# Float16 attention tiles as pairs of 64x64 products, with queries and values split as they lie

## The chip, the cores and the metric

One Trainium2 chip, one of its cores. The metric is the device time of one execution in microseconds; three executions of the kernel before are shown, and one more was taken with the profiler.

## What is computed

Attention within chunks of 64 tokens, then two feed-forward parts on its output (8 batches, 8 heads, 576 tokens, head size 64, model size 512). Cut to what matters:

```python
q_c = q.reshape(B, H, nc, 64, D); k_c, v_c likewise          # nc = 9 chunks
scores = scale * q_c @ k_c.transpose(0, 1, 2, 4, 3)           # 64 x 64 per batch, head and chunk
attn = softmax(scores); out = attn @ v_c
...
h = relu(x @ w_in); u, v = halves of h                        # first part, model size 512 -> 1024
gated = u * (w_spatial @ layernorm(v) + b_spatial); x = gated @ w_out
...
u = x + (x^T U V)^T                                           # second part
return u + relu(u @ w_ch1) @ w_ch2                            # 512 -> 2048 -> 512
```

Inputs and result are float32.

## The kernel before

Values of float32 are split into a float16 part and a float16 remainder, and a product of two such values is the sum of three float16 products: high by high, high by low, low by high. The helper `mm3` (lines 150 to 155) issues these three; each has its own weight load.

The attention has 36 tiles. A tile holds two chunks (c = 0 on partitions 0 to 63, c = 1 on partitions 64 to 127) with all 8 heads. Tiles 0 to 8 (`gen_first`) stay in float32 and are computed as pairs of 64x64 products: queries, keys and values lie on the partitions of their half, and a matmul takes partitions 0 to 63 or 64 to 127 for weights, data and output. Tiles 9 to 35 (`gen_attn`) are float16. For them the queries are written into a block-diagonal tile `qbd` (a 128x128 block per head that holds the 64x64 block of each half on its diagonal and zeros elsewhere), the values into `vbd` in the same manner, and one 128x128 weight load and one matmul with 64 moving columns serve both halves: 8 heads by 3 terms, 24 matmuls for the scores (`sp`, lines 541 to 543) and 24 for the weighted sum (`o`, lines 563 to 567). The zeros are written once, by two memsets on GpSimd (lines 888 to 891), ahead of which VectorE writes one element of each tile so that the memset waits for the seventh weight block (`after`, line 219).

`a_split_qk` and `a_split_v` (lines 358 to 379) fill these tiles: ScalarE casts the float16 part, GpSimd subtracts it for the remainder. For `qbd` and `vbd` there is one cast and one subtraction per half, of 64 partitions by 512 elements; for the keys `kd` one of each on 128 partitions. `qbd`, `vbd` and `kd` have one buffer, so the split of the next tile waits for the last matmul on this one. The row maxima, differences and sums of the softmax run on VectorE, the exponential on ScalarE; the probabilities `ph` go through a transposing DMA to `pt` and are the moving operand of the weighted sum.

Around it, `gen_dec` and `next_rest` decode the weights (loads, a scaling on ScalarE, three bit operations on VectorE at lines 183 to 187, a cast on ScalarE, a subtraction on GpSimd at line 195); `gen_moe` is the first feed-forward part, `gen_ch` the second (`phid` and `acc`). `Flow` walks the generators in a planned order of time that is set by costs such as `mmcost`; after that a scheduler orders each engine's instructions with its own model of their times. The one pin that concerns the attention is on the first score matmul of tiles 9 to 17.

Of the kernel before, what the change touches and what calls it, by code (L numbers as in the profile page):

```python
# [9 lines left out]
F16 = mybir.dt.float16  # L10
# [3 lines left out]
ALU = mybir.AluOpType  # L14
# [3 lines left out]
B, H, S, E = 8, 8, 576, 64  # L18
# [29 lines left out]
def mmcost(n, k=1):  # L48
    return k * (n / 2.4 + 2.7)
# [53 lines left out]
def moe_kernel(  # L103
# [12 lines left out]
    nc = tc.nc  # L116
    NT = q.shape[0]

    const = ctx.enter_context(tc.tile_pool(name="const", bufs=1))
# [22 lines left out]
    v4 = const.tile([128, S], F16, name="v4")  # L142
    vt2 = const.tile([128, 2, D], F16, name="vt2")
    mhalf = const.tile([128, 1], F32, name="mhalf")
    qbd = const.tile([128, 2, H, 2, 64], F16, name="qbd")
    vbd = const.tile([128, 2, 4, 2, 2, 64], F16, name="vbd")

    fl = Flow()

    def mm3(o, wh, wl, xh, xl, start, stop, pin=False):  # L150
        m = nc.tensor.matmul(out=o, lhsT=wh, rhs=xh, start=start, stop=False)  # L151
        if pin:
            tc.keep_in_program_order(m)
        nc.tensor.matmul(out=o, lhsT=wh, rhs=xl, start=False, stop=False)  # L154
        nc.tensor.matmul(out=o, lhsT=wl, rhs=xh, start=False, stop=stop)  # L155


    stage = {}

# [59 lines left out]
    def after(n, t):  # L219

        nc.vector.tensor_copy(out=t[0:1, 0:1], in_=wt[n][0:1, 1, 3, 127:128])
# [125 lines left out]
    def a_load(upto):  # L347
        while nload[0] <= min(upto, NT - 1):
            i = nload[0]
            qk = sb.tile([128, 2, 512], F32, tag="ld4", name="qk", bufs=3)  # L350
            vf = sb.tile([128, 512], F32, tag="ldv", name="vf", bufs=1)
            nc.sync.dma_start(out=qk[:, 0, :], in_=q[i])
            nc.sync.dma_start(out=qk[:, 1, :], in_=k[i])
            nc.sync.dma_start(out=vf, in_=v[i])
            ld[i] = (qk, vf)
            nload[0] += 1

    def a_split_qk(i):
        qk, vf = ld[i]
        kd = sb.tile([128, 2, H, 64], F16, tag="kd", name="kd", bufs=1)  # L360
        qv = qk[:, 0, :].rearrange("p (h t) -> p h t", h=H)
        kv = qk[:, 1, :].rearrange("p (h t) -> p h t", h=H)
        for c in range(2):
            r = slice(c * 64, (c + 1) * 64)
            nc.scalar.copy(out=qbd[r, 0, :, c, :], in_=qv[r])  # L365
            nc.gpsimd.tensor_tensor(  # L366
                out=qbd[r, 1, :, c, :], in0=qv[r], in1=qbd[r, 0, :, c, :], op=ALU.subtract)
        nc.scalar.copy(out=kd[:, 0], in_=kv)
        nc.gpsimd.tensor_tensor(out=kd[:, 1], in0=kv, in1=kd[:, 0], op=ALU.subtract)
        spl[i] = kd  # L370

    def a_split_v(i):
        vf = ld.pop(i)[1]
        nc.scalar.activation(out=vf, in_=vf, func=ACTF.Copy, scale=4.0)
        vf = vf.rearrange("p (a c e) -> p a c e", a=4, c=2)
        for c in range(2):
            r = slice(c * 64, (c + 1) * 64)
            nc.scalar.copy(out=vbd[r, 0, :, :, c, :], in_=vf[r])  # L378
            nc.gpsimd.tensor_tensor(out=vbd[r, 1, :, :, c, :], in0=vf[r], in1=vbd[r, 0, :, :, c, :], op=ALU.subtract)  # L379

    def put_tail(b):
        j = b % 2
# [3 lines left out]
    def a_softmax(sp, se=None):  # L386
        mx = sb.tile([128, H, 1], F32, tag="mx", name="mx", bufs=4)
        nc.vector.tensor_reduce(out=mx, in_=sp, op=ALU.max, axis=AXX)
        if se is None:
            se = sb.tile([128, H, 64], F32, tag="se", name="se", bufs=2)  # L390
        nc.vector.tensor_tensor(out=se, in0=sp, in1=mx.to_broadcast([128, H, 64]), op=ALU.subtract)
        nc.scalar.activation(out=se, in_=se, func=ACTF.Exp, scale=0.125)
        return se

    def a_norm(sp, se, scale):
        sm = sp[:, :, 0:1]
        nc.vector.tensor_reduce(out=sm, in_=se, op=ALU.add, axis=AXX)
        nc.vector.tensor_scalar(out=sm, in0=sm, scalar1=1e-9, scalar2=scale, op0=ALU.add, op1=ALU.mult)
        nc.vector.reciprocal(out=sm, in_=sm)
        nc.vector.tensor_tensor(out=se, in0=se, in1=sm.to_broadcast([128, H, 64]), op=ALU.mult)  # L400

    def a_out(i, o):
        p, r = divmod(i, 9)
        b = 2 * p + (r > 4)
        if r != 4:
            st = r if r < 4 else r - 5
            t0 = st * 128
            if st == 0:
                xT[b] = sb.tile([128, 2, 4, S], F16, tag="xT", name="xT", bufs=2)
                if r == 5:  # L410
                    put_tail(b)
            x = xT[b]
            nc.scalar.copy(out=x[:, 0, :, t0:t0 + 128], in_=o)
            nc.vector.tensor_tensor(
                out=x[:, 1, :, t0:t0 + 128], in0=o, in1=x[:, 0, :, t0:t0 + 128], op=ALU.subtract
            )
            fl.done(("x", b, st), 1500.0)
            return
        x = xd[p] = sb.tile([128, 2, 4, 128], F16, tag="xd", name="xd", bufs=1)
        nc.scalar.copy(out=x[:, 0], in_=o)  # L420
        nc.vector.tensor_tensor(out=x[:, 1], in0=o, in1=x[:, 0], op=ALU.subtract)
        fl.done(("x", 2 * p, 4), 2500.0)
        put_tail(2 * p)
# [100 lines left out]
    def gen_attn(lo, hi):  # L524
        if lo == 9:
            nload[0] = 9
            a_load(9)
            a_split_qk(9)
            a_split_v(9)
        for i in range(lo, hi):  # L530
            r = i % 9
            b = 2 * (i // 9) + (r > 4)
            a_load(i + 1)

            if i < 18:
                yield "until", 45000.0 + 16000.0 * (i - 9)
            kd = spl.pop(i)
            pin = True
            sp = ps_a.tile([128, H, 64], F32, tag="a", name="sp")
            qm = qbd.rearrange("p a h c t -> p a h (c t)")  # L540
            for h in range(H):
                mm3(sp[:, h, :], qm[:, 0, h, :], qm[:, 1, h, :], kd[:, 0, h, :], kd[:, 1, h, :], True, True,
                    i < 18 and h == 0)
            se = a_softmax(sp)
            if i + 1 < NT:
                a_split_qk(i + 1)
            yield "pe", mmcost(64, 24)
            yield "wait", WA
            a_norm(sp, se, float(2 ** -8))
            ph = sb.tile([128, 2, 512], F16, tag="ph", name="ph", bufs=1)  # L550
            sef = se.rearrange("p h j -> p (h j)")
            nc.scalar.copy(out=ph[:, 0, :], in_=sef)
            nc.gpsimd.tensor_tensor(out=ph[:, 1, :], in0=sef, in1=ph[:, 0, :], op=ALU.subtract)
            pt = sb.tile([128, 2, 4, 128], F16, tag="pt", name="pt", bufs=1)
            nc.sync.dma_start_transpose(
                out=pt.rearrange("p a b t -> p (a b) t"), in_=ph.rearrange("p a n -> p (a n)")
            )
            yield "wait", WB
            if r in (0, 5) and b > 1:
                yield "need", ("win", b - 2)  # L560
            o = ps_a.tile([128, 4, 128], F32, tag="a", name="o")
            vm = vbd.rearrange("p a b c x e -> p a b c (x e)")
            for hp in range(4):
                for c in range(2):
                    tt = slice(c * 64, (c + 1) * 64)
                    mm3(o[:, hp, tt], vm[:, 0, hp, c, :], vm[:, 1, hp, c, :], pt[:, 0, hp, tt], pt[:, 1, hp, tt],
                        True, True)
            a_out(i, o)
            if i + 1 < NT:
                a_split_v(i + 1)  # L570
            yield "pe", mmcost(64, 24)
            yield "wait", WC
# [291 lines left out]
    def all_of(g):  # L864
        for kind, val in g:
            if kind == "pe":
                tick(val)
# [17 lines left out]
    nc.gpsimd.memset(sp_t2, 0.0)  # L885
    nc.gpsimd.memset(u_l, 0.0)
    nc.gpsimd.memset(u_h, 0.0)
    for t in (qbd, vbd):
        u = t.rearrange("p a b c d -> p (a b c d)") if len(t.shape) == 5 else t.rearrange("p a b c d e -> p (a b c d e)")
        after(7, u)  # L890
        nc.gpsimd.memset(t, 0.0)
    all_of(gen_dec(1))
    moe = gen_moe(0)
    moe1 = None
# [16 lines left out]
    fl.t = 0.0  # L911
    fl.ev = {n: 0.0 for n in fl.ev}
    fl.add(gen_attn(9, NT), pace=0.0)

    def rest():
# [77 lines left out]
```

## Time and profile before

| | |
|---|---|
| median of three executions | 1298.79 us (1296.63 to 1301.45) |
| profiled execution | 1298.71 us, span 1296.9 us |
| TensorE matmuls busy | 1251.6 us, 97% of the span, 8612 matmuls and as many weight loads |
| VectorE, ScalarE, GpSimd busy | 507.3, 500.2, 504.5 us |
| chain that ended last | TensorE 80%, VectorE 7%, DMA 5%, GpSimd 4%, ScalarE 2%, issue 2% |
| granted TensorE clock, mean | 0.987 |

The span runs from the first to the last instruction; the 1.8 us between it and the execution's time lie around it. A matmul's row gives its start and a duration that includes the way through the array, so matmuls overlap in the rows and their distance from start to start is what the engine's time is made of. The chain is followed back from the last instruction; where it passes through an engine, that engine set the time there.

### The profile page before, as it was taken

To read this page: it belongs to the slowest core of one execution; us is meant where nothing else is said; L and a number is where in the kernel's file an instruction comes from. 1 tells how busy PE (TensorE), PEld (TensorE's weight loads), DVE (VectorE), ACT (ScalarE), POOL (GpSimd) and SP (SyncE) were. 2 spreads that over 40 slices of the span, in tenths; PEclk is the share of its full clock that TensorE was granted. 3 is DMA by queue.
4 is the path that set the end of the run, shared out by engine and by line. 5 is a ranking of instruction groups with operands and counts; after the bars stand their busy time and mean duration, and the time that the engine had idled before them with its cause. 6 is when DMAs were issued, how large, how long until landed. Compare 5 with 4: busy or idle time off the path is not lost.

```text
span 1296.9 us, 21079 instructions
## 1 busy us (share of the span) xinstructions
PE 1251.6 (97%) x8612; PEld 708.7 (55%) x8612; DVE 507.3 (39%) x934; ACT 500.2 (39%) x1024; POOL 504.5 (39%) x630
## 2 busy tenths in 40 slices
PE   7798997999999999999999999999999999999998
PEld 4476554445665466645665466545654565444443
DVE  7885777545333633242233513241114211221211
ACT  4655556445454444433354324332123212221110
POOL 4765767637455555524365515222112211020000
PEclk8799998999999999999999999999999999999999
DMA  9445335522233322420123101200011001000000
GB/s 344 154 129 137 120 115 134 123 83 53 66 78 65 90 58 50 93 67 5 34 73 71 50 1 26 45 33 5 1 28 42 1 1 28 26 17 1 33 1 33
DMA packets 95369, 81.46 MB, mean 63 GB/s; under 512 B 69668, under 2 KB 70308, under 8 KB 95272
## 3 DMA queue, kind: packets, MB, share of 16 engines
q1 hardware_dynamic: 94120, 75.92, 21.4%
q10 hardware_dynamic: 1152, 4.19, 1.0%
q8 instruction: 67, 1.10, 0.4%
q14 instruction: 30, 0.25, 0.1%
HBM read 53.62 MB, written 9.44 MB: 49 GB/s over the span
## 4 chain that ended last, share of the span: by engine, by line
PE 80%; DVE 7%; DMA 5%; POOL 4%; ACT 2%; issue 2%; SPq 0%; DVEq 0%; POOLq 0%; ACTq 0%
PE acc L151 9%; PE phid L151 9%; PE phid L155 9%; PE phid L154 9%; PE acc L155 9%; PE acc L154 9%; PE pb L151 7%; PE pb L155 7%; PE pb L154 7%; DVE dt L184 2%; DVE dt L187 2%; DMA wch<-in_q_dram 1%; DMA tr<-tr 1%; DVE dt L183 1%; POOL wch L195 1%
## 5 line engine op out<-in xcount | busy, mean ns | idle before, releaser
L824 DVE SCALAR_TENSOR_TENSOR hid<-phid,hid 128x512 f16<-128x512 f32 x144 | 99.2, 689 | 356.4 <-ACT hid L822 356.1
L151 PE MATMUL phid<-uT,wch 128*128 128x512 f16 x576 | 218.6, 379 | 1.1 <-DVE x L786 0.6
L154 PE MATMUL phid<-uT,wch 128*128 128x512 f16 x576 | 218.6, 379 | 0.0
L155 PE MATMUL phid<-uT,wch 128*128 128x512 f16 x576 | 218.4, 379 | 0.0
L154 PE MATMUL acc<-hid,wch 128*128 128x512 f16 x576 | 218.3, 379 | 0.0
L155 PE MATMUL acc<-hid,wch 128*128 128x512 f16 x576 | 218.3, 379 | 0.0
L151 PE MATMUL acc<-hid,wch 128*128 128x512 f16 x576 | 207.9, 379 | 2.2 <-ACT hid L822 2.2
L155 PEld LDWEIGHTS <-wch 128*128 128x128 f16 x1152 | 112.8, 98 | 131.4 <-issue 0.3
L151 PEld LDWEIGHTS <-wch 128*128 128x128 f16 x1152 | 112.7, 98 | 122.4 <-issue 6.5
L154 PEld LDWEIGHTS <-wch 128*128 128x128 f16 x1152 | 112.8, 98 | 117.8 <-issue 1.7
L822 ACT ACTIVATE hid<-phid 128x512 f16<-128x512 f32 x144 | 85.4, 594 | 179.7 <-PE phid L155 179.5
L683 POOL TENSOR_TENSOR gt<-g,gt 128x288 f16<-128x288 f32 x64 | 49.3, 772 | 151.7 <-ACT gt L681 151.4
L379 POOL TENSOR_TENSOR vbd<-vf,vbd 64x512 f16<-64x512 f32 x54 | 63.9, 1183 | 91.0 <-ACT vbd L378 83.7
L749 POOL TENSOR_TENSOR tr<-x,tr 128x64 f16<-128x64 f32 x64 | 48.1, 773 | 93.1 <-issue 52.1
L366 POOL TENSOR_TENSOR qbd<-qk,qbd 64x512 f16<-64x512 f32 x54 | 62.3, 1154 | 52.1 <-ACT qbd L365 48.3
L151 PE MATMUL pb<-sp_m,vn 128*128 128x288 f16 x256 | 73.2, 286 | 2.8 <-DVE hid L824 1.5
L154 PE MATMUL pb<-gt,w 128*128 128x288 f16 x256 | 73.7, 288 | 2.1 <-POOL gt L683 2.1
L151 PE MATMUL pb<-gt,w 128*128 128x288 f16 x256 | 73.5, 288 | 1.8 <-ACT tr L746 1.7
L151 PE MATMUL pb<-xT,w 128*128 128x288 f16 x256 | 73.5, 287 | 0.7 <-ACT up L659 0.7
L155 PE MATMUL pb<-gt,w 128*128 128x288 f16 x256 | 73.6, 288 | 0.0
L154 PE MATMUL pb<-xT,w 128*128 128x288 f16 x256 | 73.5, 287 | 0.0
L155 PE MATMUL pb<-xT,w 128*128 128x288 f16 x256 | 73.5, 287 | 0.0
(177 smaller groups left out, 2224.9 us busy)
## 6 DMA issues: line engine op xcount, KB each, us to landing
st<-in_wk_dram SPq DMA_DIRECT2D x24, 512.0 KB, 4.0
out_dram<-ot SPq DMA_DIRECT2D x32, 256.0 KB, 2.0
vf<-in_v_dram SPq DMA_DIRECT2D x27, 256.0 KB, 2.7
qk<-in_q_dram SPq DMA_DIRECT2D x27, 256.0 KB, 2.7
qk<-in_k_dram SPq DMA_DIRECT2D x27, 256.0 KB, 3.0
room<-in_wk_dram SPq DMA_DIRECT2D x8, 512.0 KB, 7.2
wch<-in_wk_dram ACTq DMA_DIRECT2D x8, 512.0 KB, 4.3
wch<-in_q_dram SPq DMA_DIRECT2D x9, 256.0 KB, 6.3
```

Of the source, the lines that this page charges most:

```text
L151: m = nc.tensor.matmul(out=o, lhsT=wh, rhs=xh, start=start, stop=False)
L154: nc.tensor.matmul(out=o, lhsT=wh, rhs=xl, start=False, stop=False)
L155: nc.tensor.matmul(out=o, lhsT=wl, rhs=xh, start=False, stop=stop)
L183: nc.vector.tensor_scalar(out=tb, in0=tb, scalar1=3, scalar2=None, op0=ALU.logical_shift_left)
L184: nc.vector.scalar_tensor_tensor(out=tb, in0=w[:, 0::2], scalar=29, in1=tb, op0=ALU.logical_shift_right, op1=ALU.bitwise_or)
L187: nc.vector.scalar_tensor_tensor(out=tb, in0=w[:, 1::2], scalar=0x80000000, in1=tb, op0=ALU.bitwise_and, op1=ALU.bitwise_or)
L366: nc.gpsimd.tensor_tensor(out=qbd[r, 1, :, c, :], in0=qv[r], in1=qbd[r, 0, :, c, :], op=ALU.subtract)
L379: nc.gpsimd.tensor_tensor(out=vbd[r, 1, :, :, c, :], in0=vf[r], in1=vbd[r, 0, :, :, c, :], op=ALU.subtract)
L683: nc.gpsimd.tensor_tensor(out=gt[:, 1, m, c], in0=g, in1=gt[:, 0, m, c], op=ALU.subtract)
L749: nc.gpsimd.tensor_tensor(out=th[:, o0:o0 + n], in0=x2[:, m, t0:t0 + n], in1=th[:, t0:t0 + n], op=ALU.subtract)
L822: nc.scalar.activation(out=hd[:, 0, :], in_=p, func=ACTF.Relu)
L824: nc.vector.scalar_tensor_tensor(out=hd[:, 1, :], in0=p, scalar=0.0, in1=hd[:, 0, :], op0=ALU.max, op1=ALU.subtract)
```

## The change

The block-diagonal tiles and their memsets go. Queries and values are split as they lie, into `qd` and `vd` of half the size, with one cast and one subtraction on 128 partitions each. Each of the 24 matmuls of a product becomes two with 64x64 weights, one per half, issued in turn term by term (`mm3q`).

```diff
-    qbd = const.tile([128, 2, H, 2, 64], F16, name="qbd")
-    vbd = const.tile([128, 2, 4, 2, 2, 64], F16, name="vbd")
+    qd = const.tile([128, 2, H, 64], F16, name="qd")
+    vd = const.tile([128, 2, 4, 2, 64], F16, name="vd")
...
+    halves = [slice(0, 64), slice(64, 128)]
+
+    def mm3q(parts, pin=False):
+        for n, (a, b) in enumerate(((0, 0), (0, 1), (1, 0))):
+            for p in parts:
+                m = nc.tensor.matmul(out=p[0], lhsT=p[1 + a], rhs=p[3 + b], start=n == 0, stop=n == 2)
+                if pin:
+                    tc.keep_in_program_order(m)
+                    pin = False
...
-        for c in range(2):
-            r = slice(c * 64, (c + 1) * 64)
-            nc.scalar.copy(out=qbd[r, 0, :, c, :], in_=qv[r])
-            nc.gpsimd.tensor_tensor(
-                out=qbd[r, 1, :, c, :], in0=qv[r], in1=qbd[r, 0, :, c, :], op=ALU.subtract)
+        nc.scalar.copy(out=qd[:, 0], in_=qv)
+        nc.gpsimd.tensor_tensor(out=qd[:, 1], in0=qv, in1=qd[:, 0], op=ALU.subtract)
...
-        for c in range(2):
-            r = slice(c * 64, (c + 1) * 64)
-            nc.scalar.copy(out=vbd[r, 0, :, :, c, :], in_=vf[r])
-            nc.gpsimd.tensor_tensor(out=vbd[r, 1, :, :, c, :], in0=vf[r], in1=vbd[r, 0, :, :, c, :], op=ALU.subtract)
+        nc.scalar.copy(out=vd[:, 0], in_=vf)
+        nc.gpsimd.tensor_tensor(out=vd[:, 1], in0=vf, in1=vd[:, 0], op=ALU.subtract)
...
-            qm = qbd.rearrange("p a h c t -> p a h (c t)")
             for h in range(H):
-                mm3(sp[:, h, :], qm[:, 0, h, :], qm[:, 1, h, :], kd[:, 0, h, :], kd[:, 1, h, :], True, True,
-                    i < 18 and h == 0)
+                mm3q([(sp[r2, h, :], qd[r2, 0, h, :], qd[r2, 1, h, :], kd[r2, 0, h, :], kd[r2, 1, h, :])
+                      for r2 in halves], i < 18 and h == 0)
...
-            vm = vbd.rearrange("p a b c x e -> p a b c (x e)")
             for hp in range(4):
                 for c in range(2):
                     tt = slice(c * 64, (c + 1) * 64)
-                    mm3(o[:, hp, tt], vm[:, 0, hp, c, :], vm[:, 1, hp, c, :], pt[:, 0, hp, tt], pt[:, 1, hp, tt],
-                        True, True)
+                    mm3q([(o[r2, hp, tt], vd[r2, 0, hp, c, :], vd[r2, 1, hp, c, :], pt[r2, 0, hp, tt],
+                           pt[r2, 1, hp, tt]) for r2 in halves])
...
-    for t in (qbd, vbd):
-        u = t.rearrange("p a b c d -> p (a b c d)") if len(t.shape) == 5 else t.rearrange("p a b c d e -> p (a b c d e)")
-        after(7, u)
-        nc.gpsimd.memset(t, 0.0)
```

In the changed kernel the lines behind line 155 have numbers that differ by up to 10, and the float16 products of the attention all have line 163. Of the order of instructions, two places matter.

TensorE at the scores of tile 9, the first float16 tile. Before:

```order
L676 LDWEIGHTS vt_89
L676 MATMUL pb<-sp_t_85,vt_89 128x288
L151 LDWEIGHTS qbd
L151 MATMUL sp<-kd,qbd 128x64
L154 LDWEIGHTS qbd
L154 MATMUL sp<-kd,qbd 128x64
L155 LDWEIGHTS qbd
L155 MATMUL sp<-kd,qbd 128x64
```

With the change, at the same place (the rows of `qd` alternate so 48 times):

```order
L679 LDWEIGHTS vt_89
L679 MATMUL pb<-sp_t_85,vt_89 128x288
L163 LDWEIGHTS qd
L163 MATMUL sp<-kd,qd 64x64
...
L155 LDWEIGHTS wch
L155 MATMUL phid<-uT,wch 128x512
```

The group stands where it stood, between matmuls of the full array. It has 48 loads and 48 matmuls in place of 24 and 24, and no other instruction within. So it is with all products but one weighted sum, which is cut into 14 and 34.

GpSimd near 22 to 36 us of the kernel before, where the zeros are written (`vt`, `sp_t`, `u_l` and `u_h` are other constants, `w` weight blocks). Before:

```order
L885 MEMSET sp_t_85 128x1152
L886 MEMSET u_l 128x512
L887 MEMSET u_h 128x640
L891 MEMSET qbd 128x2048
L891 MEMSET vbd 128x2048
L379 TENSOR_TENSOR vbd<-vf,vbd 64x8x64 x2
L195 TENSOR_TENSOR w_71<-dt,w_71 128x512
L195 TENSOR_TENSOR w_72<-dt,w_72 128x512
```

With the change:

```order
L888 MEMSET sp_t_85 128x1152
L889 MEMSET u_l 128x512
L890 MEMSET u_h 128x640
L205 TENSOR_TENSOR w_71<-dt,w_71 128x512
L384 TENSOR_TENSOR vd<-vf,vd 128x512
L205 TENSOR_TENSOR w_72<-dt,w_72 128x512
```

Both memsets and one of the two subtractions of tile 9's values are gone, and the subtraction of weight block 71 stands ahead of the one that is left.

## Rows read from the trace of the kernel before

**Rows 1.** Table by stretches: us, busy PE, PEld, DVE, ACT, POOL (instructions); PEclk, DMA.

```profile
125.00:250.00 125.00, 108.84 (x757) 64.72 (x755) 91.34 (x143) 72.83 (x163) 90.18 (x91) 0.97 0.49 134
250.00:1290.00 1040.00, 1037.51 (x6795) 574.08 (x6794) 317.32 (x605) 353.61 (x708) 340.92 (x453) 1.00 0.15 38
```

**Rows 2.** Grouped, TensorE from 250 us: count | busy us, mean ns | idle.

```profile
L151 PE MATMUL o<-pt,vbd 128*128 128x64 f16 x200 | 20.4, 193 | 1.3 <-DVE hid L824 1.0 <-DMA pt<-ph 0.3
...
L151 PE MATMUL sp<-kd,qbd 128*128 128x64 f16 x192 | 19.3, 193 | 0.0
```

**Rows 3.** Timeline, TensorE, scores of tile 9: start us, us, instruction, count.

```profile
186.39 0.19 PE L151 MATMUL sp<-kd,qbd 128*128 128x64 f16 x1
186.42 0.19 PE L154 MATMUL sp<-kd,qbd 128*128 128x64 f16 x1
...
187.09 0.38 PE L151 MATMUL phid<-uT,wch 128*128 128x512 f16 x1
```

**Rows 4.** Timeline, TensorE, around 64x64 float32 products of tiles 5 to 8.

```profile
51.31 0.38 PE L155 MATMUL pb<-w,xT 128*128 128x512 f16 x1
51.53 0.38 PE L151 MATMUL pb<-w,xT 128*128 128x512 f16 x1
...
53.64 0.38 PE L154 MATMUL pb<-w,xT 128*128 128x512 f16 x1
53.95 1.15 PE L514 MATMUL of<-wch 64*64 64x64 f32 x32
55.03 0.39 PE L155 MATMUL pb<-w,xT 128*128 128x512 f16 x1
...
69.54 0.29 PE L155 MATMUL pb<-xT,w 128*128 128x288 f16 x1
69.76 0.68 PE L494 MATMUL sp<-wch 64*64 64x64 f32 x16
70.37 0.30 PE L151 MATMUL pb<-xT,w 128*128 128x288 f16 x1
```

**Rows 5.** Timeline, GpSimd, 25 to 33 us.

```profile
25.39 1.80 POOL L891 MEMSET qbd<- 128x2048 f16 x1
27.13 1.80 POOL L891 MEMSET vbd<- 128x2048 f16 x1
29.66 3.21 POOL L379 TENSOR_TENSOR vbd<-vf,vbd 64x512 f16<-64x512 f32 x2 [0.73 <-ACT vbd L378]
```

**Rows 6.** Timeline, VectorE, the same weight operation twice.

```profile
26.16 0.68 DVE L184 SCALAR_TENSOR_TENSOR dt<-room,dt 128x512 uint32<-128x512 uint32 x1
...
30.21 1.65 DVE L184 SCALAR_TENSOR_TENSOR dt<-room,dt 128x512 uint32<-128x512 uint32 x1
```

**Rows 7.** Chain of waits, 20 to 36 us: start us, us, engine and line.

```profile
30.29 1.57 DVE dt L184
```

**Rows 8.** Chain of waits, 120 to 250 us.

```profile
138.38 1.16 POOL qbd L366
139.61 1.15 POOL qbd L366
...
191.93 0.53 ACT qbd L365
192.48 0.62 ACT qbd L365
...
211.77 0.52 ACT vbd L378
...
246.48 1.02 PE acc L151 x4
```

**Rows 9.** Grouped instructions, GpSimd, 125 to 247 us, by shape.

```profile
L366 POOL TENSOR_TENSOR qbd<-qk,qbd 64x512 f16<-64x512 f32 x8 | 9.2, 1150 | 0.3
...
L379 POOL TENSOR_TENSOR vbd<-vf,vbd 64x512 f16<-64x512 f32 x4 | 4.6, 1152 | 0.1
```

## Prediction

> **What bounds the kernel now.** I read the table by stretches first, then the grouped instructions of the late part, then single stretches of TensorE's timeline, then the chain of waits. The table by stretches divides the span in two. From 250 to 1290 us TensorE is busy for 1037.5 of 1040.0 us with a granted clock of 1.00, its 2.4 GHz level, while VectorE, ScalarE and GpSimd are busy for about a third of it [rows 1]. There TensorE is the bound: time added to its stream is added to the end, and time taken from the other three gives nothing. From 125 to 250 us TensorE is idle for 125.0 - 108.8 = 16.2 us, and the chain of waits runs through elementwise work until the accumulation at 246.5 us, the last piece of the chain shown [rows 1, 8]. There the other engines set the pace, and time added to TensorE largely fills its gaps. So the change has to be counted on TensorE after 246 us, and on the other three engines before.
>
> How many products lie on which side: after 250 us the first of the three terms stands 200 times for the weighted sum and 192 times for the scores, at eight to a tile: 25 + 24 = 49 products out of 54 [rows 2]. The changed order cuts one weighted sum in two, so 50 stays in the 64x64 shape lie on the bound stretch, the other five lie ahead.
>
> **What one product costs now.** The scores of tile 9 start at 186.39 us and the next, unrelated matmul at 187.09 us: 24 matmuls in 0.70 us, 29.1 ns each [rows 3]. Their weights are 128 columns, loaded anew for each matmul, and hide completely. That a row calls a matmul 0.19 us long doesn't matter; the starts do.
>
> **What one product costs after.** The stream has 48 matmuls with 48 weight loads instead of 24, in pairs on the two halves of the array. The trace has no float16 matmul of 64x64, but nine float32 tiles in that shape, and they give all the fixed costs.
> - Going in: a 512-column matmul is normally followed by the next after 0.22 us (51.31 to 51.53, more closely 215 ns); before a 64x64 group it is 0.31 us (53.64 to 53.95) [rows 4]. So the array lets the old shape run out first: 0.095 us.
> - Inside: the group at 53.95 us has 32 matmuls, 16 pairs, and the next large matmul starts 1.08 us later; the one at 69.76 us has 8 pairs and takes 0.61 us [rows 4]. The difference, 0.47 us for 8 pairs, is 58.8 ns a pair. What is left, 1.08 - 16 x 0.0588 = 0.14 us, is the first pair's weight load, which nothing hides, and the running out at the other end.
> - The large matmul behind it also can't have its weights early; I put that at 0.01 us, an estimate from the 0.39 us that it takes in place of 0.38 [rows 4].
>
> Together 0.245 us of fixed cost a product. About 0.05 us of the 0.14 is the load of the first pair (0.14 less the same 0.095 for running out); for elements of half the width I take half of it, so 0.22 us.
>
> The unknown is the distance from pair to pair in float16. Its lower end is 29.1 ns, the full-array matmul of the same type with the same 64 moving columns [rows 3]; its upper end is the float32 pair's 58.8 ns [rows 4]. If the streaming sets it, 58.8 is 128 clocks at 2.4 GHz, 53.3 ns (a float32 pair of 64 columns then takes two clocks a column), and 5.5 ns besides; float16 would take 64 clocks, 26.7 ns, and the same 5.5: 32 ns. I take 32, near the lower end, because the row of the same type is nearer in kind than the one of the same shape. Then a product takes 24 x (32.0 - 29.1) = 0.07 us more, besides the 0.22: 0.29 us. With 50 on the bound stretch: **+14.5 us**. The ends are 0.21 us (29.1 ns a pair, no exposed load to speak of) and 0.245 + 24 x 0.0297 = 0.96 us: +10.5 and +48 us.
>
> **What the other engines save.** Two half-tile casts on ScalarE become one, two subtractions on GpSimd become one, for queries and values: an operation on 64 partitions takes as long as the one that remains (1.15 us on GpSimd [rows 9]). After 250 us this hides behind TensorE and counts nothing. Before it:
> - Start. Two memsets of 1.8 us and one of the two value subtractions (3.2 us for both) leave GpSimd between 25.4 and 32.9 us [rows 5]. The chain runs there through VectorE's decoding of weights [rows 7], which is slower beside a GpSimd subtraction: 1.65 us at 30.21 for an operation that took 0.68 us at 26.16, beside a memset [rows 5, 6]. The chain doesn't name GpSimd there, and a weight subtraction moves up to where the memsets were, so I count these 0.97 us and half a microsecond for the rest, 1.5 us; bounds 0 and 5.2 (all the GpSimd time removed: 3.6 + 1.6).
> - 125 to 247 us. Six subtractions leave, half of 8 and of 4 [rows 9], 6.9 us of GpSimd. On the chain lie one of the two query subtractions at 138.4 us (1.15) and one of the two query casts at 191.9 us (0.55), and half a microsecond of value casts at 211.8 us [rows 8]: 2.2 us. The slowing of VectorE (0.97 us in the case above) I count for two of the other subtractions, 1.8 us. So 4.0; bounds 1 and 10 (all the GpSimd time and three microseconds of casts).
>
> Together **-5.5 us**, bounds 1 and 15. VectorE's two one-element copies that order the memsets go with them. The one new dependence, that a merged cast needs its whole tile free, waits for the same load and the same last matmul as the two casts before. The transposing DMAs and loads are the same in number, and the queue of SyncE takes them in a slightly different order at the start, to which I give no sign.
>
> The sum against the profiled execution: 1298.7 + 14.5 - 5.5 = 1307.7, say **1308 us**. That execution is 0.1 us under the median of the three runs shown, so no correction is due.
>
> **Rivals.**
> (1) *The weight load sets the pair's pace.* For: in the float32 group about 0.05 us of load shows at the first pair, as much as its streaming takes, so the rows can't tell which of the two made 58.8 ns [rows 4]; if a load of 64 columns takes that whatever the element's width, the float16 pair takes 58.8 ns as well. The same results if the two halves don't run at once: 2 x 29.1 = 58.2. Against: loads of 128 columns hide within 29.1 ns today [rows 3]. A product then costs 0.96 us more: 1298.7 + 48 - 5.5 = 1341 us. The Trainium skill has a rule for this side: "TensorE: Matmul & The Clock Gate", in the sections on LDWEIGHTS and on the weight path, puts a load at its columns divided by 1.2 GHz, 53 ns for 64, and grants the fast load only to full 128-column weights; "TensorEngine Tiling (Array Packing)", under feature incompatibilities, says that column tiling switches it off. By that rule it would be this rival's time; the trace agrees for the load of float32 and shows none of float16.
> (2) *The pace lies between*, 40 to 50 ns, or the start of the program is reordered for the worse: 0.5 to 0.75 us a product, 1318 to 1331 us.
> (3) *The relief ahead of 246 us outweighs the products.* GpSimd loses up to 3.6 + 1.6 + 6.9 = 12.1 us ahead of 250 us, and VectorE is slowed less often; TensorE's 16.2 us of idle time there, and more before, leave room [rows 1, 5, 9]. With the upper bound of 15 us and products at the lower one, 1298.7 + 10.5 - 15 = 1294 us. It decides from a relief of 10.5 us on; against it, only 2.2 us of the removed operations lie on the chain.
> That the change doesn't do what it says is out: the rows of the new order show 48 matmuls of 64x64 to a product.
>
> **How the numbers follow.** The forecast (pair at 29 to 34 ns, relief 2 to 10 us) spans 1301 to 1313 us and has 0.50; rival 1, 1334 to 1346 us, 0.30; rival 2, 0.10; rival 3, 0.10. Cases of both weight are far apart, so the range for 8 in 10 must take in most of both: 1299 to 1343 us; the forecast alone has 1301 to 1313. Half a per cent, about what a measurement of this kernel can tell from no change, is 6.5 us, so the line to slower is at 1305.3 us. Above it lie rivals 1 and 2 and some seven tenths of the forecast: 0.40 + 0.36 = 0.76. Faster (under 1292.3 us) is the far end of rival 3, 0.05; the rest, 0.19, is within.
>
> **What would show it.** Right: after about 245 us TensorE still without gaps, but every group of 48 matmuls of 64x64 preceded by some 0.1 us of emptiness and followed by as much; the next large matmul about 0.77 us of pairs and 0.14 us or less after the group's first. Wrong on the pace: pairs at over 50 ns, 1.4 us to a group (rival 1). Wrong on the relief: the first stretch without gaps begins over 10 us earlier than before (rival 3), or not earlier at all. Wrong altogether: consecutive large matmuls around a group at their normal distance, no running out in float16.

## The result and the profile after

| | before | after |
|---|---|---|
| median of four executions | 1298.07 us (1296.63 to 1301.45) | 1310.4 us (1309.66 to 1311.21) |
| profiled execution, span | 1298.71 us, 1296.9 us | 1309.66 us, 1307.9 us |
| granted TensorE clock, mean | 0.987 | 0.988 |

The changed kernel takes 1.0082 times as long, with a 95% interval of 1.007 to 1.0094: slower by more than half a per cent, and 2.4 us above the forecast of 1308. (The two medians alone give 1.0095, 12.3 us; the two profiled executions differ by 11.0 us. So the cost is some 11 to 12 us, and a figure that is left over from it is uncertain by a microsecond.) The mean granted clock is the same, so the clock does not explain it.

The page of the changed kernel: span, busy time of each engine (share of the span, instructions), and the engines' shares of the chain that ended last.

```profile
span 1307.9 us, 23517 instructions
...
PE 1268.2 (97%) x9908; PEld 711.2 (54%) x9908; DVE 508.3 (39%) x932; ACT 468.8 (36%) x970; POOL 433.6 (33%) x574
...
PE 80%; DVE 11%; DMA 3%; issue 2%; ACT 2%; POOL 1%; SPq 0%; DVEq 0%; ACTq 0%; POOLq 0%
```

TensorE has 1296 more matmuls. ScalarE and GpSimd lost 31 and 71 us of work, and it bought little. In the chain GpSimd fell from 4% to 1%, and VectorE, whose work is unchanged, rose from 7% to 11%.

The same two stretches as in [rows 1], in the changed kernel:

```profile
125.00:250.00 125.00, 110.56 (x863) 64.41 (x862) 93.17 (x137) 68.89 (x154) 81.83 (x83) 0.96 0.45 128
250.00:1290.00 1040.00, 1038.02 (x7910) 570.88 (x7909) 316.74 (x602) 323.41 (x658) 284.88 (x404) 1.00 0.15 39
```

From 250 us on TensorE is as full as before. In the stretch ahead of it, GpSimd is busy for 8.4 us less and TensorE's idle time went from 16.2 to 14.4 us only.

TensorE's timeline around the scores of one tile in the late part (start us, us, instruction, count), to be held against [rows 3]:

```profile
261.05 0.38 PE L151 MATMUL acc<-hid,wch 128*128 128x512 f16 x1
261.36 0.94 PE L163 MATMUL sp<-kd,qd 64*64 64x64 f16 x48
262.24 0.39 PE L154 MATMUL acc<-hid,wch 128*128 128x512 f16 x1
262.46 0.38 PE L155 MATMUL acc<-hid,wch 128*128 128x512 f16 x1
```

From the large matmul to the group it is 0.31 us, where 0.215 is normal; from the group's first matmul to the next large one 0.88 us, where it was 0.70. By the records' own starts the median group is entered 0.094 us late and takes 0.877 us in place of 0.699, and the large matmul behind it is followed by the next 0.010 us later than in the kernel before: 0.28 us more a product. The grouped instructions of TensorE from 250 us on (count | busy us, mean ns | idle):

```profile
L163 PE MATMUL o<-pt,vd 64*64 64x64 f16 x1200 | 23.8, 194 | 1.1 <-DMA pt<-ph 1.1
...
L163 PE MATMUL sp<-kd,qd 64*64 64x64 f16 x1152 | 22.7, 194 | 0.0
```

At 48 matmuls to a product that is 25 + 24 = 49 products, so 49 x 0.282 = 13.8 us. The spans differ by 11.0 us, which leaves 2.8 us for the relief (1.5 us if the medians are taken). The forecast had 14.5 and 5.5.

Where did the relief go? TensorE's waits from 125 to 250 us (line, what it waited for, us in total, times, longest), before:

```profile
PE o L151 <- DMA pt<-ph: 2.8, 1, 2.8
PE acc L151 <- ACT hid L822: 2.2, 2, 1.2
PE pb L154 <- POOL gt L683: 2.1, 1, 2.1
PE pb L727 <- ACT tr L746: 1.8, 1, 1.8
PE pb L151 <- ACT tr L746: 1.7, 1, 1.7
PE pb L151 <- DVE hid L824: 1.5, 1, 1.5
PE pb L711 <- DMA tr<-tr: 1.3, 1, 1.3
PE pb L711 <- DVE sp L397: 0.9, 1, 0.9
PE pb L151 <- ACT up L659: 0.7, 1, 0.7
PE phid L151 <- DVE x L786: 0.6, 1, 0.6
PE phid L151 <- DVE g L678: 0.5, 1, 0.5
```

and with the change:

```profile
PE pb L151 <- DVE hid L827: 3.1, 2, 2.8
PE o L163 <- DMA pt<-ph: 2.9, 2, 1.8
PE pb L714 <- DMA tr<-tr: 2.7, 2, 2.3
PE phid L151 <- DVE hid L827: 1.7, 1, 1.7
PE pb L151 <- ACT rz L636: 1.5, 1, 1.5
PE pb L786 <- DVE x L731: 1.1, 1, 1.1
PE pb L151 <- DVE g L681: 1.0, 1, 1.0
PE pb L154 <- POOL gt L686: 0.3, 1, 0.3
```

Added up by engine, waits for ScalarE and GpSimd fell from 8.5 to 1.8 us. That is 6.7 us, more than the 4.0 us forecast for this stretch. But waits for VectorE rose from 3.5 to 6.9 us and those for DMA from 4.1 to 5.6 us, so 1.8 us of it is left. Most of these 1.8 us are taken up by the five products that lie here, at 0.28 us each.

So the changed kernel's lead did not arise in this stretch. The first matmul of the second feed-forward part, before and with the change:

```profile
136.75 0.38 PE L151 MATMUL phid<-uT,wch 128*128 128x512 f16 x1 [0.59 <-DVE x L786]
134.22 0.63 PE L151 MATMUL phid<-uT,wch 128*128 128x512 f16 x1
```

A lead of 2.5 us was there already (in the traces of the runs below, with the full decoding, this matmul starts at 133.5 to 136.5 us where the first tiles have the new form throughout, and at 139.4 and 139.9 us in the edits of the kernel before), and at the 120th matmul of `acc` (248.9 and 246.7 us) it is 2.2 us. VectorE's decoding of weights got slower in between, although GpSimd had less to do beside it. Two of its five groups of bit operations from 125 to 250 us, before (x26 and x12) and with the change (x25 and x12):

```profile
L183 DVE TENSOR_SCALAR dt<-dt 128x512 uint32<-128x512 uint32 x26 | 14.5, 559 | 10.6 <-ACT dt L176 10.4
L187 DVE SCALAR_TENSOR_TENSOR dt<-wch,dt 128x512 uint32<-128x512 uint32 x12 | 12.6, 1048 | 0.2
L193 DVE TENSOR_SCALAR dt<-dt 128x512 uint32<-128x512 uint32 x25 | 15.6, 624 | 12.7 <-ACT dt L186 12.7
L197 DVE SCALAR_TENSOR_TENSOR dt<-wch,dt 128x512 uint32<-128x512 uint32 x12 | 13.2, 1101 | 0.3
```

All five together: 78 operations at a mean of 0.82 us before, 75 at 0.88 with the change. In the runs below with the full decoding it is 0.86 to 0.90 us with the new form throughout in the first tiles and 0.82 us in the edits of the kernel before, so this is no chance of one execution. Why it got slower is not shown.

### The profile page after: what moved, and what is told of

Same layout as the page of the kernel before. It is cut to its first block, busy times and chain, and to the rows that moved or that the text cites. A ratio compares the mean times of both kernels' runs of the same rounds, so it can differ in the third digit from the quotient of the medians.

```text
span 1307.9 us, 23517 instructions
## 1 busy us (share of the span) xinstructions
PE 1268.2 (97%) x9908; PEld 711.2 (54%) x9908; DVE 508.3 (39%) x932; ACT 468.8 (36%) x970; POOL 433.6 (33%) x574
## 4 chain that ended last, share of the span: by engine, by line
PE 80%; DVE 11%; DMA 3%; issue 2%; ACT 2%; POOL 1%; SPq 0%; DVEq 0%; ACTq 0%; POOLq 0%
PE acc L151 9%; PE acc L154 9%; PE acc L155 9%; PE phid L155 9%; PE phid L151 9%; PE phid L154 9%; PE pb L151 7%; PE pb L155 7%; PE pb L154 7%; DVE dt L194 3%; DVE dt L197 2%; PE o L163 2%; PE sp L163 2%; DVE dt L193 1%; ACT dt L186 1%
## 5 line engine op out<-in xcount | busy, mean ns | idle before, releaser
L151 PE MATMUL pb<-sp_m,vn 128*128 128x288 f16 x256 | 73.2, 286 | 2.1 <-ACT up L662 1.1
L155 PE MATMUL pb<-sp_m,vn 128*128 128x288 f16 x256 | 73.2, 286 | 0.0
L154 PE MATMUL pb<-sp_m,vn 128*128 128x288 f16 x256 | 73.2, 286 | 0.0
```

## The experiments

Two questions stand: what a product's 0.28 us is made of, and why the relief stayed small. All ratios are to runs of the kernel before on the same chip; a difference from the changed kernel is one between medians of separate sets of runs.

**The size by halves.** Only the scores take the new form; values, their block-diagonal tile and its memset stay as before.

```diff
+            vm = vbd.rearrange("p a b c x e -> p a b c (x e)")
...
-                    mm3q([(o[r2, hp, tt], vd[r2, 0, hp, c, :], vd[r2, 1, hp, c, :], pt[r2, 0, hp, tt],
-                           pt[r2, 1, hp, tt]) for r2 in halves])
+                    mm3(o[:, hp, tt], vm[:, 0, hp, c, :], vm[:, 1, hp, c, :], pt[:, 0, hp, tt], pt[:, 1, hp, tt],
+                        True, True)
```

> Only the scores are computed as pairs; the values keep their block-diagonal tile, memset and 24 full-array matmuls. Theory (each product in pairs costs TensorE some 0.28 us on the bound stretch: 0.22 us of running out and first load, 24 x 2.7 ns of pace): 25 products there, +7 us, less a relief of about 1 us ahead of 246 us: 1304 us, the product of the weighted sum at 0.70 us from its start to the next matmul's, that of the scores at 0.88. Rival (the cost is one of the whole program, such as more instructions to fetch, or sits in the weighted sums alone): under 1301 or about 1310.

Measured: 1305.25 us (1303.86 to 1306.15), ratio 1.005 (1.0035 to 1.0065). The score groups take 0.877 us and the weighted sums 0.699, as in the two kernels. The price goes with the number of products; half of them cost about half.

**The price of going in and out.** One full-array matmul of 64 columns, whose result is overwritten, is put into the middle of each product, first in the changed kernel, then in the kernel before.

```diff
             for h in range(H):
+                if h == 4:
+                    nc.tensor.matmul(out=sp[:, 7, :], lhsT=kd[:, 0, 0:2, :].rearrange("p h t -> p (h t)"),
+                                     rhs=kd[:, 0, 0, :], start=True, stop=True)
...
             for hp in range(4):
+                if hp == 2:
+                    nc.tensor.matmul(out=o[:, 3, 64:128], lhsT=pt[:, 0, 0, :], rhs=pt[:, 0, 0, 0:64], start=True, stop=True)
```

> The changed kernel with one more full-array matmul of 64 columns in the middle of each product (its result is written over by the next head). Theory (a change of shape makes the array run out, both ways): each of the 54 costs its own 0.03 us and 0.22 us of running out and loads; with 50 on the bound stretch 12.5 us, 1323 us, and in the timeline a distance of about 0.12 us on either side of the inserted matmul. Rival (the fixed cost comes once with a group, from its semaphores or its first loads): 50 x 0.03 = 1.5 us, 1312 us.

> Control: the kernel before with the same extra matmul in the middle of each product, where all is of the full-array shape. Both theories: 50 x 0.03 us = 1.5 us, 1300 us, distances of 29 ns on both sides. If it costs over 5 us, the inserted matmul itself waits for something and the run with it in the changed kernel says nothing of shapes.

Measured: in the changed kernel 1321.7 us (1320.93 to 1324.12), ratio 1.0181 (1.0165 to 1.0196), 11.3 us above the change. In the kernel before 1300.64 us, ratio 1.0017 (1.0008 to 1.0026). TensorE's timeline of the first of the two:

```profile
401.91 0.56 PE L163 MATMUL sp<-kd,qd 64*64 64x64 f16 x24
402.41 0.20 PE L547 MATMUL sp<-kd 128*128 128x64 f16 x1
402.54 0.56 PE L163 MATMUL sp<-kd,qd 64*64 64x64 f16 x24
403.04 0.30 PE L154 MATMUL pb<-gt,w 128*128 128x288 f16 x1
```

The product takes 1.13 us in place of 0.88: one small matmul costs 0.25 us when the array has to change its shape for it twice, and 0.03 us (0.728 against 0.699) when it need not. So the fixed price lies in the change of shape, both ways.

**Does the streaming set the pace?** In the second and third of the three terms the matmuls stream 32 columns in place of 64: first with both halves of the array, then with one half alone; and, for comparison, with both halves, in the full-array matmuls of the kernel before (its edit, the same by a parameter of `mm3`, is not shown).

```diff
         for n, (a, b) in enumerate(((0, 0), (0, 1), (1, 0))):
             for p in parts:
-                m = nc.tensor.matmul(out=p[0], lhsT=p[1 + a], rhs=p[3 + b], start=n == 0, stop=n == 2)
+                w = 64 if n == 0 else 32
+                m = nc.tensor.matmul(out=p[0][:, 0:w], lhsT=p[1 + a], rhs=p[3 + b][:, 0:w], start=n == 0, stop=n == 2)
```

The one with one half has besides:

```diff
-            for p in parts:
+            for p in (parts if n == 0 else parts[:1]):
```

> The changed kernel with 32 instead of 64 moving columns in the second and third term (half of the two correction terms is left out); as many loads of 64 weight columns as before. If the streaming sets the pairs' pace: 16 of 24 pairs go from 31.8 to some 18.5 ns, 0.21 us less a product, 10.6 us in all, 1300 us. If the load of 64 weight columns sets it: the distance stays near 31.8 ns and the time near 1310 us. In between (a floor of 25 ns): 1305 us.

> The changed kernel with the second and third term for the first half only and with 32 moving columns (two thirds of the second half's terms and some of the first half's are left out). Two lone matmuls follow each pair, each with one load of 64 weight columns. If the load of 64 columns sets the pace: some 29 to 32 ns for a lone matmul as for a pair, product from its start to the next matmul still near 0.86 us. If the number of instructions sets it (four to a pair in 31.8 ns, 8 ns each): 16 ns for a lone matmul, product near 0.6 us.

> The kernel before with 32 instead of 64 moving columns in the second and third term of the attention's float16 products (half of the correction terms is left out). If the full-array load of 128 columns is shorter than the streaming of 64 (26.7 ns): distances fall from 29.1 towards 16 ns for these matmuls, a product from 0.70 to about 0.49 us. If it is that load that sets the 29.1 ns: no change.

The changed kernel with half the columns takes 1310.58 us (ratio 1.0094, 1.0077 to 1.0111), as without the edit. With one half alone it is 1304.36 us in one execution, but its groups are the same again; the groups explain under 1 us of the difference, and what made the rest stays open. TensorE's timeline, half the columns:

```profile
400.18 0.93 PE L164 MATMUL sp<-kd,qd 64*64 64x64 f16 x48
401.04 0.30 PE L154 MATMUL pb<-gt,w 128*128 128x288 f16 x1
```

and one half alone:

```profile
414.11 0.93 PE L164 MATMUL sp<-kd,qd 64*64 64x64 f16 x32
414.97 0.39 PE L154 MATMUL acc<-hid,wch 128*128 128x512 f16 x1
```

Both groups take 0.86 us, with 48 matmuls or with 32. From pair to pair, and from lone matmul to lone matmul, it stays 31.7 ns. In the kernel before (1299.9 us in one execution) the product went from 0.699 to 0.639 us, so its short matmuls came 25.6 ns apart where they had come 29.1 ns apart, neither unchanged nor at half. So in the 64x64 shape neither the streaming nor the number of matmuls sets the pace, and a pair costs what one matmul of it costs. What is left is the weight load or a fixed price of a step.

**The load, or a fixed price?** The score products take 32 weight columns on each half (a full-array matmul ahead of the group fills the rest of the tile), or 128 weight columns on partitions 0 to 63 alone, one matmul a step.

```diff
+    quarters = [slice(0, 32), slice(64, 96)]
...
-                mm3q([(sp[r2, h, :], qd[r2, 0, h, :], qd[r2, 1, h, :], kd[r2, 0, h, :], kd[r2, 1, h, :])
-                      for r2 in halves], i < 18 and h == 0)
+                mm3q([(sp[r2, h, :], qd[r4, 0, h, 0:32], qd[r4, 1, h, 0:32], kd[r4, 0, h, :], kd[r4, 1, h, :])
+                      for r2, r4 in zip(quarters, halves)])
```

```diff
-                mm3q([(sp[r2, h, :], qd[r2, 0, h, :], qd[r2, 1, h, :], kd[r2, 0, h, :], kd[r2, 1, h, :])
-                      for r2 in halves], i < 18 and h == 0)
+                w2 = [qd[halves[0], a, h // 2 * 2:h // 2 * 2 + 2, :].rearrange("p h t -> p (h t)") for a in range(2)]
+                mm3q([(sp[:, h, :], w2[0], w2[1], kd[halves[0], 0, h, :], kd[halves[0], 1, h, :])],
+                     i < 18 and h == 0)
```

> All score products take 32 weight columns in place of 64 on each half of the array, so half of the scores are left to one matmul of the full array ahead of the group, which fills the whole score tile with products of the keys; moving columns and the number of matmuls stay. Theory, that the load of the weight columns sets the 31.8 ns from pair to pair: the pairs come at 26 ns or less and a group of 48 takes 0.74 us or less from its first matmul to the next large one, in place of 0.88. Rival, that a step in this shape has a fixed price whatever its weights: 31.8 ns and 0.88 us as in the changed kernel. The weighted sums are unchanged and stay at 0.88. The whole run is no measure here: 24 added matmuls of 512 columns, 0.22 us each, make some 5 us more, against 3.4 us less by the theory.

> The score products use the queries and keys of partitions 0 to 63 alone, with two heads' queries as 128 weight columns: 24 matmuls of 64 rows by 128 columns in place of 24 pairs, so the scores of the second half and the pairing of heads are left wrong. Theory, that the load of the weight columns sets the pace: twice the columns, about 58 ns a step (2 x 26.7 + 5), a group of 1.4 to 1.5 us, some 14 us more in all. Rival, a fixed price of a step in a divided array: 31.8 ns, 0.88 us a group, no change in all. Third possibility: the slow load hangs on the divided columns alone, and 128 columns in one piece load as fast as in the full array: 26 to 29 ns a step, 0.75 to 0.81 us.

One execution each, 1310.78 and 1306.26 us. TensorE's timeline, 32 weight columns:

```profile
417.16 0.38 PE L546 MATMUL sp<-kd 128*128 128x512 f16 x1
417.47 0.87 PE L164 MATMUL sp<-kd,qd 64*32 64x64 f16 x48
418.28 0.39 PE L154 MATMUL phid<-uT,wch 128*128 128x512 f16 x1
```

and 128 weight columns:

```profile
417.13 0.87 PE L163 MATMUL sp<-kd,qd 64*128 64x64 f16 x24
417.94 0.39 PE L154 MATMUL acc<-hid,wch 128*128 128x512 f16 x1
```

Both groups take 0.81 us and both have steps of 29.2 ns, next to the full array's 29.1. A fixed price of 31.8 ns is refuted by both. My theory as written ("26 ns or less") fell too: I had left out that 64 moving columns took 29 ns in the full array too. With 128 columns the third possibility came true. Put together, a step with 64 moving columns takes 29 ns, or 31.7 ns where the weights are 64 columns wide. That it is their load, and not another price of this width, is read from the first step of a group, where less of it is hidden: from the first matmul to the first of the second pair it is 52 ns with 64 weight columns and 39 ns with 32. The weight loads' own records agree: from a group's first load to the first load of the second pair it is 28 ns with 64 columns, 15 ns with 32. The 13 ns for 32 columns are 0.41 ns a column, an estimate of 26 ns for a load of 64 if the time grows evenly with the columns; the other 5 ns of the 31.7 are not explained. With 128 columns the first step is 39 ns and the second load starts 15 ns after the first, so a piece of 128 columns loads faster than one of 64.

**Is the relief worth having by itself?** The new form for tiles 9 to 12 alone, whose products lie mostly ahead of 250 us; from tile 13 on the block-diagonal form, its memsets at that place (the splits and the weighted sums switch in the same manner).

```diff
+    LIM = 13
...
+                if i < LIM:
+                    mm3q([(sp[r2, h, :], qd[r2, 0, h, :], qd[r2, 1, h, :], kd[r2, 0, h, :], kd[r2, 1, h, :])
+                          for r2 in halves], i < 18 and h == 0)
+                else:
+                    mm3(sp[:, h, :], qm[:, 0, h, :], qm[:, 1, h, :], kd[:, 0, h, :], kd[:, 1, h, :], True, True,
+                        i < 18 and h == 0)
```

> Pairs only for tiles 9 to 12, which run mostly ahead of 246 us where the other engines set the pace; from tile 13 on block-diagonal tiles, whose two memsets move there. Theory (the pairs cost 0.28 us each on the stretch where TensorE is the bound, and the smaller splits help only ahead of it): keeps the 2 us that the changed kernel is ahead at 250 us, pays 3 or 4 products, 1 us: 1297 to 1298 us, under both kernels. Rival (the changed kernel's lead at 250 us is chance of its order): 1299 to 1302 us.

Measured: 1299.55 us (1298.19 to 1301.95) against 1299.14, ratio 1.0004 (0.9995 to 1.0013). The relief by itself gives nothing that can be measured. (Three of its products lie past 250 us and cost 0.8 us, so a relief of up to 1.5 us would still fit the interval.) TensorE's timeline has one of the waits in which it ended:

```profile
235.50 1.49 PE L168 MATMUL o<-pt,vbd 64*64 64x64 f16 x48 [1.82 <-DMA pt<-ph]
```

A weighted sum waits 1.82 us for the transposing DMA of its probabilities.

**Does VectorE's decoding set the pace ahead of 250 us?** For 32 weight blocks VectorE leaves out the middle one of its bit operations, in the changed kernel, in the kernel before and in the one with the new form for four tiles alone.

```diff
-        nc.vector.scalar_tensor_tensor(
-            out=tb, in0=w[:, 0::2], scalar=29, in1=tb, op0=ALU.logical_shift_right, op1=ALU.bitwise_or
-        )
+        if not (isinstance(name, int) and name >= 12):
+            nc.vector.scalar_tensor_tensor(
+                out=tb, in0=w[:, 0::2], scalar=29, in1=tb, op0=ALU.logical_shift_right, op1=ALU.bitwise_or
+            )
```

> The changed kernel without the middle one of VectorE's three operations for the 32 weight blocks of the second feed-forward part (leaves out their three lowest mantissa bits). Theory (with GpSimd and ScalarE relieved, VectorE's decoding sets the pace from 125 to 246 us, so the relief was taken up there): 32 operations of 0.7 to 1.5 us less, TensorE without gaps some 5 to 15 us earlier, 1297 to 1305 us. Rival (loads or GpSimd set the pace there, or the plan's order does): within 2 us of the changed kernel, 1308 to 1311 us.

> The kernel before without the same VectorE operation for the 32 weight blocks of the second feed-forward part (leaves out their three lowest mantissa bits). The changed kernel gained 14.6 us by this. If VectorE's decoding set the pace before the change as well: 12 to 15 us less here too, 1284 to 1287 us. If GpSimd with its doubled subtractions was close behind: only 6 to 11 us, 1288 to 1293 us, and the difference to 14.6 us is what the lighter GpSimd is worth once VectorE is out of the way.

> Pairs for tiles 9 to 12 alone (as in the hybrid) and without that VectorE operation (the three lowest mantissa bits of the 32 blocks are left out). If the lighter GpSimd and ScalarE help only when VectorE isn't the bound: 2 to 6 us under the kernel before with the same omission. If they never help: equal to it within 1.5 us.

| less decoding in | median | ratio to before | against the same kernel with it |
|---|---|---|---|
| the changed kernel | 1295.81 us | 0.9973 (0.9963 to 0.9984) | -14.6 us |
| the kernel before | 1286.28 us | 0.9893 (0.9878 to 0.9908) | -13.7 us |
| four tiles in the new form | 1287.39 us | 0.9901 (0.9885 to 0.9918) | -12.2 us |

The stretch from 125 to 250 us with less decoding, in the changed kernel:

```profile
125.00:250.00 125.00, 120.50 (x1021) 70.67 (x1020) 73.70 (x121) 75.21 (x166) 82.17 (x89) 0.99 0.46 132
```

and in the kernel before:

```profile
125.00:250.00 125.00, 118.92 (x882) 70.58 (x881) 73.88 (x121) 79.02 (x173) 87.01 (x95) 0.99 0.47 138
```

VectorE is busy for 17 to 20 us less there, and TensorE's idle time falls from 14 to 16 us to 4.5 and 6.1 us. So VectorE's work sets the pace of this stretch in both kernels, and taking work from GpSimd beside it frees little. At most 2 to 4 of the 14 us are the granted clock, which is 0.99 in this stretch in place of 0.97 and 0.96. Even with less decoding the new form for four tiles doesn't pay: 1287.39 against 1286.28 us, within 1.1 us. Its waits of TensorE from 250 to 500 us say where its lead went:

```profile
PE o L156 <- DMA pt<-ph: 4.1, 4, 1.6
PE sp L156 <- DVE xT L442: 0.6, 1, 0.6
```

In the kernel before with less decoding, the same stretch has a single wait:

```profile
PE o L151 <- DVE ast L717: 1.2, 1, 1.2
```

TensorE comes early to weighted sums whose probabilities are still in the transposing DMA. The fastest of all is the kernel before with less decoding, but it leaves out the three lowest mantissa bits of those weights; no version here is faster and computes the whole.

## Why the prediction was right, and where its steps failed

- **Where the bound lies: right.** From 250 us on nearly all of a product's price reached the end: the 5520th matmul from the end (those of the float16 products not counted) starts at 274.8 us before and at 273.3 us with the change; from there on, with 47 products in each kernel, the changed one takes 12.5 us longer, 0.27 us a product. Ahead of 250 us the other engines set the pace.
- **Number and price of the products: right in size.** 49 products at 0.28 us, 13.8 us, for 50 at 0.29, 14.5 us. Of the 0.28 us, the running out on the way in is 0.094 us (0.095 forecast), the first step, with its load uncovered, 0.023 us more than a step before, the 22 other steps 22 x (31.67 - 29.13) = 0.056 us, the way out 0.099 us, and the next large matmul 0.010 us (0.01 forecast). The extra full-array matmul shows the two ways as a cost of their own. The float32 groups of [rows 4] were a good measure of float16's.
- **The pace: right number, wrong reason.** "If the streaming sets it" gave 32 ns; it measured 31.7 ns. But half the moving columns left it as it was, and 32 or 128 weight columns took it to 29.2 ns, so the 64 weight columns set it, by their load as the first steps show. That 32 and 31.7 ns agree is luck. This was rival 1's mechanism. Rival 1 priced that load at the float32 pair's 58.8 ns; a float16 step, load included, measured 31.7 ns. What decided between 1308 and 1341 us was the load's length in float16, for which the trace before had no row. The rule named with that rival, in "TensorE: Matmul & The Clock Gate" of the Trainium skill (section on LDWEIGHTS), would have 53 ns for 64 columns; the measured step of 31.7 ns, with one load on each half in it, contradicts that figure. That weights of full 128 columns load fast, as the same page of the Trainium skill says in its section on the weight path, agrees with the 29.2 ns at 128 columns.
- **The relief: the step that failed.** "So 4.0" and "1.5 us" at the start; together 2.8 us came out of the 5.5 (1.5 by the medians), and not where it was booked: 2.5 us of lead stood at 134 us already, and the stretch that was to give 4.0 us gave about what its five products cost. Counting the removed query and value operations on the chain [rows 8] was right as far as it went: the waits for GpSimd and ScalarE fell by 6.7 us. The failure is that nothing was put in their place. Waits for VectorE were next, 3.4 us longer, and those for DMAs, 1.5 us. The other half of the term, 1.8 us for a VectorE that is slowed less, had the wrong sign: its decoding took 0.06 us more an operation, over 4 us in 75 operations.
- **Rival 3**, a relief of over 10.5 us, was far off: VectorE's work ahead of 250 us is the same in both kernels.
- The two errors, 0.7 us too much on the products and 2.7 us too much on the relief, go opposite ways in the sum; 1307.7 stands against 1309.7 us of the profiled execution.

On VectorE's slowing at the start, the chain of waits of the changed kernel has this row, which answers to [rows 7]:

```profile
31.14 1.49 DVE dt L194
```

and GpSimd's timeline has at the same time the subtraction of values that is left:

```profile
30.93 1.16 POOL L384 TENSOR_TENSOR vd<-vf,vd 128x512 f16<-128x512 f32 x1
```

The operation took 1.57 us in the chain before and takes 1.49 now: it runs beside a GpSimd subtraction in both kernels, so the 0.97 us booked for it did not come. Another operation did gain, which the forecast had not looked at. VectorE's first bit operation of a weight block ran beside the second memset before [rows 5] and has no GpSimd work beside it now (VectorE's timeline, before and with the change):

```profile
27.35 1.86 DVE L183 TENSOR_SCALAR dt<-dt 128x512 uint32<-128x512 uint32 x1
27.83 0.41 DVE L193 TENSOR_SCALAR dt<-dt 128x512 uint32<-128x512 uint32 x1
```

From 20 to 60 us the 18 decoding operations take 13.4 us in place of 17.0. Whether that made the lead of 2.5 us at 134 us is not shown: the run with the scores alone in the new form, which saves one memset, reaches the same matmul at 142.2 us, later than either kernel, so the order of the work counts there too.

What stays open: the 5 ns of a step beyond the estimated load, why VectorE's decoding got slower from 125 to 250 us, and how much of the wait for the transposing DMA could be had back by another order of the work, which wasn't tried.

## What to carry to other kernels

Dividing the array for products that sit between full-array work cost a fixed 0.23 us each time here, besides the work inside, so count the changes of shape before the zeros that are saved. Before a relief on one engine is booked, add up the waits by engine in that stretch and ask which engine is late next; from 125 to 250 us nearly three quarters of what left GpSimd's and ScalarE's account came back on VectorE's and the DMAs'. A forecast whose number rests on an untested "if" should be tested at the "if" even when the number comes true, since half the columns looked like a saving by that "if" and were none.

## What the runs showed of the hardware

- A pair of 64x64 float16 matmuls on the two halves of the array costs what one of them costs alone: 31.7 ns a step either way.
- A step with 64 weight columns (31.7 ns) is slower than one with 32 or with 128 (29.2 ns each), all with 64 moving columns.
- Halving the moving columns from 64 to 32 took the full-array matmul from 29.1 to 25.6 ns only.
- One full-array matmul between 64x64 ones costs 0.25 us, and 0.03 us among its own kind.
- A uint32 VectorE operation of 128x512 that takes 0.41 us elsewhere took 1.86 us beside a GpSimd memset; another kind, beside a memset, kept its 0.68 us and took 1.49 to 1.65 us beside a GpSimd subtraction.
